# Strassen's scheme for the first large product of an attention-and-MoE kernel, from the third token block on

## The chip, the cores and the metric

The kernel runs on one core of one Trainium2 chip. The metric is device time in microseconds of one execution, lower is better; a time that is given for a kernel is the median of its runs. The core has a matrix engine (TensorE, "PE" in the profile, with its weight loads apart as "PEld"), VectorE (DVE), ScalarE (ACT), GpSimd (POOL) and SyncE (SP), which here issues nearly all transfers. Each engine works through its own list of instructions in order, and the engines wait for each other by semaphores. TensorE writes its results to PSUM, eight banks of 512 float32 columns on 128 partitions; the other data lie in SBUF.

## The reference

An attention without a score matrix feeds a two-layer network without experts' routing. All is float32.

```python
q_s = softmax(q over head_dim);  k_s = softmax(k over seq)      # (8 batches, 8 heads, 576, 64)
kv  = einsum('bhsd,bhse->bhde', k_s, v)                         # 64 x 64 for each head
att = einsum('bhsd,bhde->bhse', q_s, kv)
x   = att.transpose(0, 2, 1, 3).reshape(4608, 512)              # a token's heads side by side
h   = x @ w_in                                                  # 512 -> 2048
r   = maximum(h, 0)
g   = s * (r * r) + b
out = g @ w_out                                                 # 2048 -> 512
```

## The kernel before

**Precision.** TensorE takes its operands in a rounded float32 form (F32R). To keep float32 accuracy each operand is split into a high part and the rest: `xh`, `xl` for x, `gh`, `gl` for g, and two halves for each weight. A product is then three matmuls: high by high, high by rest, rest by high.

**Tiling.** The 4608 tokens are nine blocks of 512: block b of the first eight holds 512 of the 576 tokens of batch b, and the ninth holds the 64 that are left of each batch, which go through a DRAM buffer (`xleft`) and are loaded back at the end (`left_over`, line 699). The 2048 columns of w_in are sixteen chunks of 128 (`NFC`). A step t is one block and one chunk, 144 steps in all. It has twelve matmuls for h (`h_parts`, line 726: four chunks of 128 of the 512 inputs, three matmuls each, 512 tokens wide), then the path through relu, square, scale and bias to `gh` and `gl` (`step`, lines 770 to 791: ScalarE 770 and 787, VectorE 785 and 789), and twelve matmuls for the outputs (`o_parts`, line 814: four tiles of 128 tokens, three matmuls each, 512 output columns wide). The outputs of a block accumulate in four PSUM banks over its sixteen steps and leave through `leave` (line 819).

**Weights.** Block 0 loads each chunk of w_in and w_out, cleans and splits it (`conv_w`, line 189), and keeps it in SBUF for all later blocks, w_in's part in `wt[f][:, 0]`.

**Attention.** The x of batches 2 to 7 is made while the big products of earlier blocks run. For a pair of units (a unit is two heads) it loads k, q and v, takes maxima, exponentials and sums, turns q through DRAM, and multiplies: `kv_late` (line 629) gives the 64 x 64 matrices, `x_late` (line 658) gives x. In `x_late` line 676 has four matmuls per unit, two of 320 and two of 256 columns, into a two-bank PSUM tile ("big") and a one-bank one ("sm"); lines 682 and 686 add the halves into `y` by a ScalarE copy and a VectorE sum, and lines 690 and 694 split `y` into `xh` and `xl`. GpSimd takes the subtraction and the scaling of q (575 and 592) and a split of kv (656).

**What sets the order.** The order of instructions is written by a planner (`Order`, line 114). Each stream of work is a generator that yields operations `Op(engine, cost, due, needs, take, free, gives)`. The planner keeps a time per engine, takes the operation that could start first and, among those of the same engine that could start within 0.1 us of it, the one with the smallest `due`. `take` and `free` count buffers ("h" and "big" are PSUM tiles, "g" the pairs of gh and gl, "w" the weight slots), `needs` and `gives` are results. Costs and dues are constants in the code. `begin(pr)` (line 530) is the due of a pair of attention: the first step of its own block, or six steps later for the second pair. The result is one fixed list per engine, SP's list of transfers included.

## Time and profile before

| | before |
|---|---|
| runs | 871.24, 872.84, 873.27 us; median 872.84 |
| profiled execution, span from first to last instruction | 869.5 us |
| TensorE busy | 851.7 us (98%) |
| VectorE, ScalarE, GpSimd busy | 570.8, 416.3, 91.4 us |
| bytes moved | 79.44 MB, mean 91 GB/s |
| granted TensorE clock | 1.000 |

The span is of one profiled execution; no separate time of that execution outside the profile is listed, so it stands beside the runs' times, which are 2 to 4 us longer. "Busy" is the union of an engine's instructions. Matmuls are pipelined and their ends modelled, so a matmul's listed length is longer than the distance from its start to the start of the next; distances between starts tell what TensorE spends. The chain that ended last follows the work back from the last instruction to what released it. A "releaser" of an idle time is what the engine waited for by the semaphores; idle time of an engine off that chain costs nothing.

### The profile page before, as it was taken

Reading aid. Unit: us, or ns where it says so; the run is one execution under the profiler, and the core shown is the slowest. Engines: PE = TensorE matmul, PEld = TensorE weight load, DVE = VectorE, ACT = ScalarE, POOL = GpSimd, SP = SyncE. Lnnn points to the kernel's source line nnn. Section 1 sums busy time; section 2 is a strip of 40 time slices with the busy share of each in tenths; the row PEclk is TensorE's granted clock in tenths of the full one; section 3 lists DMA queues with packets and bytes.
Section 4 is the critical chain, followed back from the end, with each engine's and each line's share of the span. In section 5 each row is a group of like instructions: output and inputs, shape, how many; then the busy total and the mean of one; then the engine's idle time right before and its main releaser. Section 6 shows DMA issues by size and latency. Waiting matters only on the chain.

```text
span 869.5 us, 11637 instructions
## 1 busy us (share of the span) xinstructions
PE 851.7 (98%) x4367; PEld 701.9 (81%) x4367; DVE 570.8 (66%) x916; ACT 416.3 (48%) x694; POOL 91.4 (11%) x117
## 2 busy tenths in 40 slices
PE   7799999999999999999999999999999999999997
PEld 6578887888888888888888888888888888888886
DVE  6999997596877777686677658785855322232222
ACT  5989864544554545353545354444544322222222
POOL 1000002021102111111021202020200010000000
PEclk9999999999999999999999999999999999999999
DMA  8994134424433334342433242432311000000001
GB/s 232 308 378 136 26 86 118 127 74 97 137 82 89 83 119 100 90 92 78 130 89 83 89 130 75 96 89 82 77 61 52 33 16 1 1 30 19 1 1 48
DMA packets 109991, 79.44 MB, mean 91 GB/s; under 512 B 60656, under 2 KB 103664, under 8 KB 109808
## 3 DMA queue, kind: packets, MB, share of 16 engines
q1 hardware_dynamic: 108496, 77.60, 31.8%
q10 hardware_dynamic: 1440, 1.12, 0.4%
q8 instruction: 34, 0.56, 0.3%
q14 instruction: 21, 0.17, 0.1%
HBM read 60.29 MB, written 18.40 MB: 91 GB/s over the span
## 4 chain that ended last, share of the span: by engine, by line
PE 92%; DVE 4%; DMA 1%; SPq 1%; issue 1%; ACT 0%; ACTq 0%; DVEq 0%
PE acc L814 44%; PE h L726 44%; PE kv L299 2%; PE xp L676 1%; PE xq L676 1%; DMA k<-in_k_dram 1%; DVE low L216 1%; DMA st<-in_moe_w_in_dram 0%; DVE st L213 0%; PE xp L440 0%; DVE w L223 0%; DMA v<-in_v_dram 0%; SPq L288 0%; DVE low L206 0%; DVE st L211 0%
## 5 line engine op out<-in xcount | busy, mean ns | idle before, releaser
L726 PE MATMUL h<-x,w 128*128 128x512 f32 x1728 | 420.2, 391 | 2.4 <-ACT r L770 1.2
L726 PEld LDWEIGHTS h<-x,w 128*128 128x128 f32 x1728 | 322.7, 188 | 71.6 <-ACT r L770 1.9
L814 PE MATMUL acc<-w,gh 128*128 128x512 f32 x1152 | 357.8, 392 | 0.8 <-ACT gh L780 0.8
L814 PEld LDWEIGHTS acc<-w,gh 128*128 128x128 f32 x1152 | 214.0, 188 | 45.6 <-ACT gh L780 1.2
L785 DVE SCALAR_TENSOR_TENSOR r<-r,sb 128x512 f32<-128x512 f32 x135 | 106.1, 786 | 190.1 <-ACT r L770 189.7
L814 PE MATMUL acc<-w,gl 128*128 128x512 f32 x576 | 224.5, 390 | 0.6 <-DVE gl L782 0.6
L770 ACT ACTIVATE r<-h 128x512 f32<-128x512 f32 x143 | 85.5, 598 | 277.3 <-PE h L726 264.9
L789 DVE SCALAR_TENSOR_TENSOR gl<-r,sb,gh 128x512 fp32r<-128x512 f32 x135 | 104.5, 774 | 56.5 <-ACT gh L787 55.2
L787 ACT ACTIVATE gh<-r,sb 128x512 fp32r<-128x512 f32 x135 | 97.7, 724 | 84.8 <-DVE r L785 84.4
L814 PEld LDWEIGHTS acc<-w,gl 128*128 128x128 f32 x576 | 108.1, 188 | 23.8 <-DVE gl L782 1.1
L575 POOL TENSOR_TENSOR q<-q,qm 128x640 f32<-128x640 f32 x24 | 33.7, 1406 | 161.4 <-DVE qm L573 161.4
L592 POOL TENSOR_TENSOR qe<-qe,qr 128x640 f32<-128x640 f32 x24 | 32.3, 1347 | 65.8 <-DVE qr L588 43.7
L682 ACT COPY y<-xp 64x320 f32<-64x320 f32 x48 | 20.2, 420 | 13.8 <-PE xp L676 13.4
L686 DVE TENSOR_TENSOR y<-xp,y 64x320 f32<-64x320 f32 x48 | 23.5, 489 | 3.4 <-ACT y L682 2.5
L562 ACT ACTIVATE k<-k 128x640 f32<-128x640 f32 x24 | 17.7, 737 | 15.1 <-DVE k L524 12.3
L596 DVE STREAM_TRANSPOSE q<-qe 128x640 f32<-128x640 f32 x24 | 19.9, 831 | 5.2 <-POOL qe L592 5.2
L299 PEld LDWEIGHTS kv<-v,k 128*64 128x64 f32 x600 | 18.7, 137 | 5.1 <-issue 4.4
L656 POOL TENSOR_TENSOR spare<-kvf,spare 128x256 fp32r<-128x256 f32 x12 | 10.1, 844 | 118.6 <-issue 112.8
L613 DVE TENSOR_TENSOR qhl<-qT,qhl 64x640 fp32r<-64x640 f32 x24 | 20.6, 860 | 1.1 <-ACT qhl L610 0.4
L686 DVE TENSOR_TENSOR y<-xq,y 64x256 f32<-64x256 f32 x48 | 20.3, 422 | 1.0
L299 PE MATMUL kv<-v,k 128*64 128x65 f32 (+1 forms) x600 | 20.8, 224 | 0.0
L200 ACT ACTIVATE low<-st 128x1024 int32<-128x1024 uint32 (+1 forms) x17 | 18.9, 1111 | 3.2 <-DVE w L223 1.9
(124 smaller groups left out, 619.6 us busy)
## 6 DMA issues: line engine op xcount, KB each, us to landing
st<-in_moe_w_in_dram SPq DMA_DIRECT2D x16, 512.0 KB, 8.7
st<-in_moe_w_out_dram SPq DMA_DIRECT2D x16, 512.0 KB, 9.1
out_dram<-o SPq DMA_DIRECT2D x16, 512.0 KB, 2.7
turned<-q SPq DMA_DIRECT2D x24, 320.0 KB, 2.3
qT<-turned SPq DMA_DIRECT2D x48, 160.0 KB, 3.0
k<-in_k_dram SPq DMA_DIRECT2D x14, 512.0 KB, 4.2
q<-in_q_dram SPq DMA_DIRECT2D x14, 512.0 KB, 5.3
v<-in_v_dram SPq DMA_DIRECT2D x56, 128.0 KB, 4.8
```

Source lines behind the costliest of these rows:

```text
L299: nc.tensor.matmul(kv[h * D:(h + 1) * D, i], kt[:, i, h, n], vt[:, 2 * i + h, n], start=(n == 0), stop=(n == NT - 1))
L575: nc.gpsimd.tensor_tensor(out=qt, in0=qt, in1=bc(qm, [P, 2, NT, D]), op=ALU.subtract)
L592: nc.gpsimd.tensor_tensor(out=qe_, in0=qe_, in1=qr, op=ALU.mult)
L613: nc.vector.tensor_tensor(out=t[half[1 - h], h], in0=qT[half[h]], in1=t[half[h], h].bitcast(F32), op=ALU.subtract)
L682: nc.scalar.copy(y[half[h], at], parts[h][a][half[1 - h]])
L686: nc.vector.tensor_tensor(out=y[half[h], at], in0=parts[h][a][half[h]], in1=y[half[h], at], op=ALU.add)
L726: nc.tensor.matmul(hp_, w[:, j, c, :], x[:, c, :], start=(c == 0 and i == 0), stop=(c == NP - 1 and i == 2))
L770: nc.scalar.activation(r, hp_, AF.Relu)
L785: nc.vector.scalar_tensor_tensor(out=r, in0=r, scalar=s_col, in1=r, op0=ALU.mult, op1=ALU.mult)
L787: nc.scalar.activation(gh, r, AF.Identity, bias=b_col)
L789: nc.vector.scalar_tensor_tensor(out=gl, in0=r, scalar=b_col, in1=gh.bitcast(F32), op0=ALU.add, op1=ALU.subtract)
L814: nc.tensor.matmul(acc[blk, j // 2][:, j % 2], g[:, js], w_, start=(f == 0 and i == 0), stop=(f == NFC - 1 and i == 2))
```

## The change

From block 2 on (`PLAIN = 2`, blocks counted from 0) the h of two chunks, a pair, is computed together. The 512 inputs, the 256 columns of w_in and the 512 tokens are each cut in two, and the four half-by-half blocks of h are formed out of seven products in place of eight, in the Winograd form of Strassen's scheme. A product is six matmuls of 256 columns. Its left side is one of A11, A12, A22 (parts of w_in) or S1 to S4 (sums of them), its right side one of B11, B21, B22 (parts of x) or T1 to T4 (sums of them).

- *Sums of w_in.* In block 1 the needed parts are stored to DRAM (`keep_parts`), the sums are made from them and stored too (`combine`: VectorE two sums, GpSimd four of half width, ScalarE two high parts, GpSimd two rests, for each of eight pairs of chunks). The weight slots of w_in become free slots. In blocks 2 to 8 each product's left side is loaded again from DRAM, two products per transfer of 512 KB (`stream`), at most six transfers ahead (`KEPT`). The slots (16 of the weights, 4 of an x buffer, less one that serves as a third g) hold these loads and the x parts.
- *Sums of x.* `prepare` takes the place of lines 688 to 694: from `y` it makes B and T parts and their splits, on VectorE, ScalarE and GpSimd.
- *Products.* One two-bank PSUM tile, `hset`, has four quarters of 256 columns. The seven products go to quarters 3, 2, 1, 3, 3, 0, 2. Quarter 3 is copied away by ScalarE three times in a pair, after the products 1, 3 and 4 (results u1, u2, u3); products 0 to 6 wait for these and for the row sums.
- *Rows.* `rows_a` adds u3 to quarters 1 and 2 (first chunk), `rows_b` adds u1 and u2 to quarters 0 and 2 (second chunk), on VectorE from PSUM. `square` then does relu and square in one VectorE instruction, scale and bias and gh on ScalarE, gl on GpSimd. Before, this was two ScalarE and two VectorE instructions for a chunk.
- *Outputs.* Same matmuls as before, as a stream of their own with due t + 9; g has three buffers.
- *Attention.* Its dues become a list, `DUE_B`. From block 3 on `x_late` does a unit in two halves with one-bank PSUM tiles "h" and "sm", because `hset` now keeps "big".

The diff, cut to its core:

```diff
+    DUE_S = (11.0, 12.0, 17.0, 17.0, 26.0, 20.5, 26.0, 69.5)
+    DUE_B = (7.5, 8, 16, 28.0, 43.5, 47.0, 55.5, 60, 69.5, 80.0, 81.5, 107.5)
+    S_ON = ('POOL', 'POOL', 'POOL', 'POOL', 'POOL', 'POOL')
+    X_ON = ('POOL', 'POOL', 'POOL', 'DVE', 'POOL', 'DVE')
+    G_ON = ('POOL', 'POOL')
+    DUE_G = -16.0
+    DUE_R = (-16.0, -18.0)
+    DUE_O = 9.0
+    DUE_ST = 2.5
+    PLAIN = 2
+    HP, OPS = NFC // 2, 7
+    KEPT = 6
...
-        bb, hq = divmod(pr, NP // 2)
-        return NFC * bb + PACE * hq
+        return DUE_B[pr - NP]
...
+            for h in range(2):
+                yield Op("PE", 0.29, due - NFC, needs=needs, take=["h", "sm"], gives=[f"xp{u}"] * h, late=WAIT)
...
+                yield Op("ACT", 0.79, due, take=() if h else ["tmp"])
...
+                yield Op("DVE", 0.91, due, free=["h", "sm"], gives=[f"y{u}"] * h)
...
+    def prepare(bb, c, y, due, free, gives):
+        kt, M = c % 2, TB // 2
+        K = raw["K"][:, kt]
+        if c < 2:
+            yield Op("ACT", 0.36, due, needs=["late"])
+            nc.scalar.copy(K[:, M:TB], y[:, 1])
+            yield Op("DVE", 0.42, due)
+            nc.vector.tensor_tensor(out=y[:, 1], in0=y[:, 1], in1=y[:, 0], op=ALU.subtract)
+            yield Op("ACT", 0.6, due, take=["pc"])
+            t = pair_sum(bb, c, "X0")
+            nc.scalar.copy(both(t[:, 0]), y)
...
+            by(X_ON[c]).tensor_tensor(out=both(t[:, 1]), in0=y, in1=both(t[:, 0]).bitcast(F32), op=ALU.subtract)
+            return
+        yield Op("DVE", 0.7, due)
+        nc.vector.tensor_tensor(out=both(K), in0=y[:, 1].unsqueeze(1).to_broadcast([P, 2, M]), in1=both(K), op=ALU.subtract)
...
+    ORDER = ("A11", "S1", "A22", "S2", "S3", "A12", "S4")
+    WITH = {"A11": "B11", "S1": "T1", "A22": "T4", "S2": "T2", "S3": "T3", "A12": "B21", "S4": "B22"}
...
+    def combine(i):
...
+        for j, g in enumerate((f + 1, f)):
+            yield Op("DVE", 0.7, due, needs=["late", f"w{g} 0"], take=() if j else ["F"])
...
+        for n, (out_, x, y, op) in enumerate(sums):
+            yield Op(S_ON[n], on(S_ON[n], 0.85, 0.42), due)
+            by(S_ON[n]).tensor_tensor(out=out_, in0=x, in1=y, op=op)
...
+    def stream(m):
...
+        yield Op("SP", 0.65, NFC * blk + 2 * uses[0][0] + DUE_ST, needs=needs, take=["pc", "ahead"], kb=512, gives=[f"s{m}"])
+        W[m] = slot()
+        nc.sync.dma_start(W[m].bitcast(F32), ws[n].rearrange("p o l e -> p o (l e)"))
...
+    def products(p):
...
+        before = {
+            0: [f"u3 {p - 1}", f"P{OPS - 1} {p - 1}", f"o{t - 3} {NQ - 1}"], 1: [f"row1 {p - 1}"], 2: [f"row2 {p - 1}"], 3: [f"u1 {p}"], 4: [f"u2 {p}"], 5: [f"row2 {p}"], 6: []
+        }
...
+        where = (3, 2, 1, 3, 3, 0, 2)
+        for k, name in enumerate(ORDER):
...
+            yield Op(
+                "PE", 0.71, t - 1, needs=before[k] + x_needs(blk, x) + [f"s{m}"], take=["big"] if p == 0 and k == 0 else (),
+                free=free + ["pc"] * len(gone), gives=[f"P{k} {p}"] + ([f"h{t}", f"h{t + 1}"] if k == OPS - 1 else [])
+            )
...
+            for kt in range(2):
+                xs = x_of(blk, x, kt)
+                for a, b_ in ((0, 0), (0, 1), (1, 0)):
+                    nc.tensor.matmul(out_, w[:, a, kt], xs[:, b_], start=k in (0, 2) and n == 0, stop=n == 5, skip_group_check=True)
+                    n += 1
...
+    def square(t, row, due, eng, free):
+        yield Op("DVE", 0.79, due)
+        nc.vector.scalar_tensor_tensor(out=row, in0=row, scalar=0.0, in1=row, op0=ALU.max, op1=ALU.mult)
+        yield Op("ACT", 0.73, due)
+        nc.scalar.activation(row, row, AF.Identity, bias=b_col, scale=s_col)
+        yield Op("ACT", 0.57, due, take=["g"])
+        G[t] = gh, gl = raw["g"][t % 3]
+        nc.scalar.copy(gh, row)
+        yield Op(eng, on(eng), due, free=free, gives=[f"g{t}"])
+        by(eng).tensor_tensor(out=gl, in0=row, in1=gh.bitcast(F32), op=ALU.subtract)
...
+    def rows_a(p):
...
+        for n, k in enumerate((1, 3, 4)):
+            yield Op("ACT", 0.38, due, needs=[f"P{k} {p}"], gives=[f"u{n + 1} {p}"])
+            V, U = raw["V"][p % 2], raw["U"]
+            nc.scalar.copy(U if n == 2 else V[:, n * M:(n + 1) * M], hset[0][:, 3 * M:4 * M])
+        yield Op("DVE", 0.72, due, needs=[f"P2 {p}"], take=["r"], gives=[f"row2 {p}"])
...
+    def outputs(t):
...
+            yield Op(
+                "PE", 0.68, t + DUE_O, needs=[f"g{t}", f"o{t - 1} {j}"],
...
-            + [step(t) for t in range(NSTEP)]
+            + [step(t) for t in range(PLAIN * NFC)]
+            + [late_()] + [g(i) for g in (keep_parts, combine) for i in range(HP)] + [stream(m) for m in range(NPAIR * OPS // 2)]
+            + [g(p) for p in range(NPAIR) for g in (products, rows_a, rows_b)] + [outputs(t) for t in range(PLAIN * NFC, NSTEP)]
```

The steps of blocks 0 and 1 keep their instructions; `DUE_G` gives those of block 1 an earlier due on ScalarE and VectorE.

More of the change, by code (lines that the diff above doesn't have):

```diff
@@ L741, in step @@
         first = blk == 0
+        due = t + (-2 if first else DUE_G)
         parts = h_parts(t)
@@ L748, in step @@
             hp_ = next(parts)
-        yield Op("ACT", 0.5, t - 2, take=["r", "g"], free=["h"] if t < NSTEP - 1 else ())
+        yield Op("ACT", 0.5, due, take=["r", "g"], free=["h"] if t < NSTEP - 1 else ())
         r, gh, gl = g_tiles(t)
```

255 lines of the change are left out of this document (214 added, 41 removed).

## The prediction

> **What bounds the kernel now.** I read the page first: its busy shares, its transfer rates in 40 slices and its chain of work that ended last.
>
> ```profile
> span 869.5 us, 11637 instructions
> PE 851.7 (98%) x4367; PEld 701.9 (81%) x4367; DVE 570.8 (66%) x916; ACT 416.3 (48%) x694; POOL 91.4 (11%) x117
> GB/s 232 308 378 136 26 86 118 127 74 97 137 82 89 83 119 100 90 92 78 130 89 83 89 130 75 96 89 82 77 61 52 33 16 1 1 30 19 1 1 48
> PE 92%; DVE 4%; DMA 1%; SPq 1%; issue 1%; ACT 0%; ACTq 0%; DVEq 0%
> ```
>
> TensorE is the chain. The profiled execution spans 869.5 us and the runs' median is 872.84, so 3.3 us lie around the span; I make the sum on the span and add 3.3. Next, the chain in order of time (start, length), and windows over blocks 1, 2 and 4 (counted from 0), cut where a block's first h starts.
>
> ```profile
> 138.84 2.72 PE h L726 x12
> 141.56 2.72 PE acc L814 x12
> ```
>
> ```profile
> core 0: us, PE busy (x) PEld busy (x) DVE busy (x) ACT busy (x) POOL busy (x), PEclk, DMA share, GB/s
> 131.91:225.60 93.69, 93.69 (x485) 77.34 (x485) 71.43 (x120) 47.19 (x81) 17.42 (x17) 1.00 0.37 95
> 225.60:317.96 92.36, 92.36 (x482) 76.56 (x480) 68.68 (x117) 43.88 (x77) 14.58 (x15) 1.00 0.38 105
> 410.32:502.68 92.36, 92.36 (x482) 76.56 (x480) 65.69 (x112) 43.16 (x76) 13.91 (x14) 1.00 0.34 92
> ```
>
> Twelve matmuls of 512 columns take 2.72 us, 226.7 ns each; a step is 24 of them, 5.44 us, and sixteen steps are 87.04 of a block's 92.36 us; the rest is attention's matmuls. Two blocks with different vector work agree to 0.01 us: nothing but TensorE sets their length. VectorE has 24 us free in block 2, ScalarE 48, GpSimd 78. So a cut in matmul columns is worth its full time, as long as what Strassen adds elsewhere stays below what is free and does not reach TensorE as a wait.
>
> **What a half-width matmul costs.** The change turns 24 matmuls of 512 columns (h of two chunks) into seven products of six matmuls of 256. The kernel before has 48 matmuls of 256 columns, in attention's x product (L676, "xq"), between ones of 320. TensorE's timeline, the first unit and the end of the last:
>
> ```profile
> 172.18 0.31 PE L676 MATMUL xp<-qhl,spare 128*128 128x320 f32 x1
> 172.33 0.28 PE L676 MATMUL xq<-qhl,spare 128*128 128x256 f32 x1
> 172.45 0.31 PE L676 MATMUL xp<-qhl,spare 128*128 128x320 f32 x1
> 172.59 0.28 PE L676 MATMUL xq<-qhl,spare 128*128 128x256 f32 x1
> 172.71 0.39 PE L814 MATMUL acc<-w,gh 128*128 128x512 f32 x1
> ```
>
> ```profile
> 660.05 0.28 PE L676 MATMUL xq<-spare 128*128 128x256 f32 x1
> 660.17 0.62 PE L726 MATMUL h<-x,w 128*128 128x512 f32 x2
> ```
>
> Starts count, since the lengths hold a modelled drain. From a 256-column start to the next it is 0.12; the mean of all 48 is 0.118. That is more than half of 226.7 (113.3): part of a matmul does not shrink with its columns. I take 0.118, the row of the same width and type, and keep 0.1133 as the lower end. Each of these matmuls has a weight load of its own, hidden at this spacing, so the larger number of loads costs nothing more. The Trainium skill, "TensorE: Matmul & The Clock Gate", section "Back-to-back issue gap", gives N/2.4 + 2.5 ns for a warm matmul, 216 ns at 512 columns; the trace disagrees with its 226.7. By the page's 109 ns at 256 columns the result would be about 832 us.
>
> Removed per pair of chunks: 24 x 0.2267 = 5.44. Added: 42 x 0.118 = 4.96. Saved: 0.484. Seven blocks of eight pairs are 56 pairs: **-27.1 us**. The pair then lasts 10.4 us with its outputs, and a block 88.5.
>
> **What is added beside TensorE.** From the groups (the number behind the busy time is the mean in ns), then from the view of line 785 and of the tile y (min/median/max):
>
> ```profile
> L785 DVE SCALAR_TENSOR_TENSOR r<-r,sb 128x512 f32<-128x512 f32 x135 | 106.1, 786 | 190.1 <-ACT r L770 189.7
> L770 ACT ACTIVATE r<-h 128x512 f32<-128x512 f32 x143 | 85.5, 598 | 277.3 <-PE h L726 264.9
> L789 DVE SCALAR_TENSOR_TENSOR gl<-r,sb,gh 128x512 fp32r<-128x512 f32 x135 | 104.5, 774 | 56.5 <-ACT gh L787 55.2
> L787 ACT ACTIVATE gh<-r,sb 128x512 fp32r<-128x512 f32 x135 | 97.7, 724 | 84.8 <-DVE r L785 84.4
> L656 POOL TENSOR_TENSOR spare<-kvf,spare 128x256 fp32r<-128x256 f32 x12 | 10.1, 844 | 118.6 <-issue 112.8 <-ACT spare L654 5.8
> L694 DVE TENSOR_TENSOR x<-y,x 128x512 fp32r<-128x512 f32 x24 | 20.1, 838 | 0.0
> L449 DVE TENSOR_TENSOR x<-xp,x 128x512 fp32r<-128x512 f32 x8 | 5.5, 681 | 1.6 <-ACT xleft L241 1.4
> L780 ACT CAST gh<-r 128x512 fp32r<-128x512 f32 x8 | 4.9, 618 | 0.2
> L712 POOL TENSOR_TENSOR x<-xleft_all,x 128x512 fp32r<-128x512 f32 x4 | 5.4, 1338 | 72.5 <-ACT x L710 72.5
> ```
>
> ```profile
> L785 DVE SCALAR_TENSOR_TENSOR r<-r,sb x135: 651/753/1459, 38.2 to 854.2; 128x512 f32<-128x512 f32 x135
> ```
>
> ```profile
> L682 ACT COPY y<-xq x48: 363/368/373, 173.7 to 661.5; 64x256 f32<-64x256 f32 x48
> L686 DVE TENSOR_TENSOR y<-xq,y x48: 415/422/428, 176.3 to 662.6; 64x256 f32<-64x256 f32 x48
> L694 DVE TENSOR_TENSOR x<-y,x x24: 628/684/1752, 179.6 to 666.0; 128x512 fp32r<-128x512 f32 x24
> ```
>
> VectorE, block 2 to 5 (mean of the two windows 67.2 us). Removed: 16 x (0.786 + 0.774) = 25.0, and four xl at 0.838, 3.4. Added: 16 row sums from PSUM (nearest L449, 0.681) and 16 squarings (L785's median, 0.753), 22.9; the sums of x, by L694's median and L686: two chunks at 0.42, two at 0.684 + 2 x 0.42, two splits at 0.684, 5.3. That leaves 67.0 in 88.5: no more than before. ScalarE loses 2 x (0.598 + 0.724) and gains three copies at 0.368 and 2 x (0.724 + 0.618) per pair, 1.1 us more, 9 a block beside 44 busy. GpSimd gains 16 + 4 operations at 1.338, 26.8 a block beside 14. All three stay off the path. The sums of w_in are made in block 1 for all pairs: per pair 2 x 0.684 on VectorE (10.9 in all), 4 x 0.844 + 2 x 1.338 on GpSimd (48.4), on ScalarE two casts; VectorE's 71.43 in 93.69 becomes 82.4. Cost nothing, as the steps of block 1 are unchanged and TensorE hides it; if VectorE were full, each us over 93.69 would be lost (first rival). The split of attention's x product into halves, the second waiting until copy and add have emptied the bank, costs TensorE the same four matmuls; its wait is hidden by outputs and products, at worst 0.37 + 0.42 in each of 20 units, 16 us; I take nothing, since queued outputs are ready then.
>
> Waits for TensorE. A product's quarter of the PSUM tile must be emptied before the next use. The end of the kernel shows the hand-over:
>
> ```profile
> 856.06 2.88 PE L726 MATMUL h<-x,w 128*128 128x512 f32 x12
> 858.78 0.39 PE L814 MATMUL acc<-w,gh 128*128 128x512 f32 x1
> ```
>
> ```profile
> 858.98 0.66 ACT L757 ACTIVATE r<-h 128x256 f32<-128x256 f32 x2 [3.30 <-PE h L726]
> ```
>
> ScalarE starts 0.20 after TensorE's next slot begins. So product 4 follows product 3 after 0.20 + 0.37 = 0.57 at the least, less than one output tile (3 x 0.2267 = 0.68); product 5 follows 4 after 0.20 + 0.37 + 0.68 = 1.25 (two tiles); the next pair's product 1 follows this pair's 6 after 0.88, of which product 0 covers 0.71. The loop of products alone is 4.96 + 0.57 + 1.25 + 0.17 = 6.95 of 10.4 us, so 3.4 us a pair are left for queueing behind other work on ScalarE and VectorE (operations of 0.4 to 0.8, five hand-overs), and the outputs wait behind nothing but g. Bounds: none (block 2 to 5 as they are now), or five full operations of 0.8 against 3.4, 0.6 a pair, over the 40 pairs of blocks 2 to 6 that share with attention 24 us. I take 5, nearer to the rows of now: **+5.0**. Below nothing it can't go, as these blocks wait for nothing now.
>
> Pipeline ends. Filling at step 32: products of pair 0 have the outputs of steps 30 and 31 between them, but the first new g comes 4 us after its row: none, to one step's outputs (2.72); **+1.0**. At the end the last row's chain is 0.20 + 0.68 + 0.75 + 0.72 + 0.62 + 1.34 = 4.31, with five hand-overs of 0.04 (below) 4.5, against 2.72 of outputs and two matmuls (0.45) that need gh alone: **+1.3**.
>
> Streams: 3.5 loads of 512 KB in 10.4 us are 176 GB/s on top of 105, 281; in block 1 the 56 stores of 256 KB are 157 GB/s on top of 95, 252; slice 2 of the page moved 378. Off the path, at nothing; late loads are the second rival. New waits hold up what stands behind them: on TensorE, behind a waiting product, the outputs planned after it, and so the g buffers that ScalarE fills; on SP, behind a load that waits for a slot, attention's loads.
>
> Sum: -27.1 + 5.0 + 1.0 + 1.3 = -19.8; 849.7 span, **853.0 us**.
>
> **Rivals.** *GpSimd blocks VectorE* (slower). From the timeline:
>
> ```profile
> 147.13 2.95 POOL L592 TENSOR_TENSOR qe<-qe,qr 128x640 f32<-128x640 f32 x2 [2.56 <-PE h L726]
> ```
>
> ```profile
> 147.67 1.27 DVE L785 SCALAR_TENSOR_TENSOR r<-r,sb 128x512 f32<-128x512 f32 x1 [0.38 <-ACT r L770]
> 148.98 0.73 ACT L787 ACTIVATE gh<-r,sb 128x512 fp32r<-128x512 f32 x1 [1.34 <-DVE r L785]
> ```
>
> A squaring started under a GpSimd operation takes 1.27 in place of 0.753. The Trainium skill, "SBUF — State Buffer", section "Who interferes with whom", says that a VectorE instruction with two SBUF inputs and a GpSimd one that reads SBUF exclude each other, whichever came first; by that rule the trace agrees (1.27), and it speaks against this change. If all new GpSimd time blocked VectorE, block 1 would need 82.4 + 48.4 = 130.8 (+37.1) and blocks 2 to 5 67.0 + 26.8 = 93.8 (+5.3 each, 21): 853.0 - 5.0 + 58 = 906. It decides from about three quarters: block 1 then loses 25.0, as much as the 24.8 left of the gain. Against it: the waits now, 135 x 0.033 at L785 and 24 x 0.154 at L694, are 8.2 us, 9% of GpSimd's 91.4. Chance 0.07.
>
> *Streams late* (slower). The queue's own waits:
>
> ```profile
> SPq L509 <- DVE top L504: 106.5, 12, 13.7
> ```
>
> SP stands up to 13.7 us, 8.9 on average, and loads queue behind that. A load lasts 10.4 / 3.5 = 3.0 us of products: six ahead are 18, enough. If slots let only two be ahead, 12 waits each cost 8.9 - 6 = 2.9, 35 us: 883. It loses from about 2.3 ahead. Against it: twenty slots, and SP takes these waits when it has nothing else. Chance 0.05.
>
> *Copies and sums come late, part of the gain*: 0.4 us a pair over 40 pairs in place of 5.0, 16: 864. For it: five hand-overs a pair where there was one a step; against it the 3.4 us. Chance 0.15.
>
> *Half the columns, half the time*: 42 x 0.1133 = 4.76, saved 0.68, 38.1: 842. Against it the 0.12 between starts. Chance 0.07. The 832 us by the Trainium skill's page on TensorE, above, lie on this side, 10 us further. That fewer products are not made is no case: seven names, six matmuls each, stand in the code.
>
> **How the numbers follow.** Forecast 0.66, with 848 (no waits) to 860 as its own range; late copies 0.15, half time 0.07, blocked 0.07, late streams 0.05. 842 to 867 holds all but the last two and a margin. About 0.3% (2.6 us) is what a measurement tells from no change: faster 0.66 + 0.07 + 0.13 = 0.86, same 0.04, slower 0.10.
>
> **What would show it.** Right: 256-column starts 0.118 apart, 2352 of them, block windows of 88.5 to 89.5 from block 2 on, VectorE near 67 in blocks 2 to 5, the last two blocks shortest. Wrong: PE idle before products ended by ACT or DVE (late copies, and where VectorE's operations are stretched, the lock), by a DMA (streams), block 1 longer than 94 (sums of w_in), or starts under 0.115.

## The result, and the profile after

The changed kernel takes 909.0 us (four runs, 907.4 to 909.5) against 872.4 for the kernel before in runs beside it (four, 871.2 to 873.3): 1.042 times the time before, with a 95% interval of 1.040 to 1.043. It is slower by 37 us where the prediction had it faster by 20. The page of the changed kernel, its first lines and its chain by engine:

```profile
span 907.3 us, 14713 instructions
...
PE 860.1 (95%) x5375; PEld 733.4 (81%) x5375; DVE 660.3 (73%) x976; ACT 510.3 (56%) x932; POOL 339.6 (37%) x301
...
PE 70%; DVE 15%; ACT 6%; issue 3%; DMA 3%; POOL 2%; SPq 1%; DVEq 0%; POOLq 0%; ACTq 0%
```

TensorE held 92% of the chain before and holds 70% now; VectorE went from 4% to 15%. So the chain now runs through other engines for a larger part, that is, TensorE stands more often. Where it stands shows in the windows by block, cut where a block's outputs end (blocks 1 to 4, 7 and 8; columns as in the windows of the prediction):

```profile
137.90:247.55 109.65, 101.10 (x494) 80.39 (x492) 96.12 (x137) 54.40 (x99) 57.57 (x49) 0.95 0.62 168
247.55:356.95 109.40, 100.81 (x695) 86.47 (x694) 93.44 (x136) 62.27 (x121) 66.08 (x55) 0.98 0.85 259
356.95:451.14 94.19, 91.93 (x625) 79.99 (x624) 76.23 (x118) 54.79 (x108) 40.68 (x34) 1.00 0.82 246
451.14:545.62 94.48, 91.67 (x625) 79.95 (x624) 75.01 (x118) 55.18 (x108) 42.23 (x34) 1.00 0.83 247
728.92:817.21 88.29, 85.91 (x530) 75.55 (x528) 34.44 (x44) 37.82 (x70) 28.02 (x21) 1.00 0.52 176
817.21:901.98 84.77, 81.54 (x487) 70.75 (x485) 23.65 (x30) 30.26 (x53) 19.39 (x15) 1.00 0.37 132
```

Cut the same way, the kernel before has 92.36 in each of blocks 1 to 6, and in blocks 7 and 8:

```profile
692.84:779.90 87.06, 87.06 (x386) 72.07 (x384) 26.48 (x33) 24.12 (x38) 5.35 (x4) 1.00 0.03 13
779.90:864.61 84.71, 84.71 (x373) 69.48 (x371) 25.40 (x35) 21.75 (x35) 0.00 (x0) 1.00 0.04 14
```

Blocks 1 and 2 lose 17 us each, and not one later block gains more than 2.2 us (block 5, 90.22), though each has its eight pairs of cheaper products. In blocks 1 and 2 VectorE is busy for 96 and 93 us and the granted clock (the column after GpSimd's) is below 1.

A ledger of TensorE's time helps to keep these apart. It goes by the distances between starts of matmuls: the usual distance of a width belongs to the matmul, what is over it by more than 0.03 is a wait, and what is over it at half clock stands by itself. The last column is an experiment that is told below. The sums leave out some 7.6 us at the end of each execution, behind the last matmul.

| TensorE, us | before | after | e9: three causes removed |
|---|---|---|---|
| h and products | 392.3 | 368.2 | 367.6 |
| outputs | 392.3 | 396.6 | 396.7 |
| attention | 52.5 | 52.8 | 53.7 |
| waits | 24.9 | 74.4 | 40.6 |
| half clock | 0 | 7.6 | 3.4 |

The products did save 24.1 us. Against that waits grew by 49.5, half clock by 7.6, the outputs by 4.3 and attention by 0.3. That makes 37.6, of the 37.8 by which the span grew.

**The waits.** The list of waits, TensorE's weight loads (what waited, for what, us in total, times, longest; the weight load takes a wait first, so its list is the fuller one):

```profile
PEld hset L948 <- ACT late L984: 31.9, 92, 1.1
PEld hset L948 <- DVE row L987: 8.5, 8, 2.6
PEld acc L1117 <- DVE gl L1092: 5.3, 3, 2.5
PEld xp L718 <- DVE y L678: 4.4, 6, 1.6
```

No DMA is among the larger ones: the streamed sums of w_in come in time. The first row is products waiting for L984, the copy of quarter 3 of `hset`. It is there even in the last two blocks, where attention is gone. One pair of block 8 in TensorE's and ScalarE's timeline, products 0 and 1, product 2, the copy u1, product 3, an output tile:

```profile
862.33 1.60 PE L948 MATMUL hset<-w,w 128*128 128x256 f32 x12
...
863.76 0.88 PE L948 MATMUL hset<-slots,w 128*128 128x256 f32 x6
864.68 0.37 ACT L984 COPY late<-hset 128x256 f32<-128x256 f32 x1 [1.52 <-PE hset L948]
...
865.10 0.62 PE L948 MATMUL hset<-w,w 128*128 128x256 f32 x3 [0.46 <-ACT late L984]
...
865.92 0.63 PE L1117 MATMUL acc<-w,gh 128*128 128x512 f32 x2
...
866.39 0.39 PE L1117 MATMUL acc<-w,gl 128*128 128x512 f32 x1
```

ScalarE had been idle for 1.52 us and yet the copy began at 864.68, 0.20 after product 2's end (863.76 + 6 x 0.12 = 864.48), not 0.20 after product 1's at 863.76. Product 3 therefore waits 865.10 - 864.48 = 0.62 us. The planner's list says that u1 needs product 1 (`enumerate((1, 3, 4))`), and orders the work for that. The built kernel does otherwise: in 54 of the 56 pairs u1 starts after product 2's last matmul, though that writes quarter 1 in the other bank; in the two others it starts before product 2 does. This is as if dependences were kept for a PSUM tile as a whole and counted for what is emitted earlier; e5 below puts that to the test. In 22 pairs nothing stands between the products 2 and 3, and in 20 of them TensorE waits 0.62 us or a little more (the other two are those whose copy came early), 12.5 us in all. Such a pair lasts 11.3 us, and 10.6 where the wait is gone (e5 below).

**VectorE stretched.** The groups of the squaring, one for each row of a pair:

```profile
L967 DVE SCALAR_TENSOR_TENSOR late<-late 128x512 f32<-128x512 f32 x56 | 62.5, 1116 | 1.3
L967 DVE SCALAR_TENSOR_TENSOR row<-row 128x512 f32<-128x512 f32 x56 | 45.6, 814 | 1.2
```

The same instruction takes 0.81 us in the mean for one row and 1.12 for the other, which comes while GpSimd makes the first row's gl. Summed over all of VectorE's instructions, the time over each group's fast ones (its tenth percentile) is 98.6 us in blocks 1 to 8, against 15.6 before; 41 of them fall in blocks 1 and 2.

**Half clock.** Five stretches of 3.4 us have a granted clock of 0.5; the kernel before has none until its matmuls are done. Two windows from ahead of such stretches, then the two stretches themselves (the second column of the busy times is TensorE's weight load, the column after GpSimd's the clock):

```profile
195.50:198.90 3.40, 1.03 (x4) 0.30 (x2) 3.28 (x7) 1.30 (x3) 1.05 (x1) 1.00 0.87 279
250.10:253.50 3.40, 1.00 (x7) 0.80 (x7) 3.30 (x6) 1.75 (x4) 1.04 (x2) 1.00 0.70 235
```

```profile
198.90:202.30 3.40, 3.28 (x8) 2.61 (x9) 2.61 (x5) 1.32 (x2) 2.50 (x3) 0.50 0.71 192
253.50:256.90 3.40, 3.40 (x16) 3.40 (x17) 0.65 (x1) 2.35 (x4) 2.42 (x3) 0.50 0.76 238
```

In each of the first two windows lies one of the longest waits of the list above (2.5 for L1092, 2.6 for L987), and 3.4 us at half clock follow: a long wait can be paid again. One of the five stretches (38.4) lies in block 0, ahead of all sums and products; e6's execution below has none there.

### The profile page after: what moved, and what is told of

Its sections match the earlier page's. It is cut to its first block, busy times and chain, and to the rows that moved or that the text cites. A ratio compares the mean times of both kernels' runs of the same rounds, so it can differ in the third digit from the quotient of the medians.

```text
span 907.3 us, 14713 instructions
## 1 busy us (share of the span) xinstructions
PE 860.1 (95%) x5375; PEld 733.4 (81%) x5375; DVE 660.3 (73%) x976; ACT 510.3 (56%) x932; POOL 339.6 (37%) x301
## 3 DMA queue, kind: packets, MB, share of 16 engines
q10 hardware_dynamic: 1440, 1.12, 0.4%
## 4 chain that ended last, share of the span: by engine, by line
PE 70%; DVE 15%; ACT 6%; issue 3%; DMA 3%; POOL 2%; SPq 1%; DVEq 0%; POOLq 0%; ACTq 0%
PE acc L1117 34%; PE hset L948 27%; PE h L1028 6%; PE kv L311 2%; DVE late L967 1%; ACT late L984 1%; DVE y L678 1%; DVE qs L593 1%; DVE row L987 1%; DVE late L775 1%; DVE late L998 1%; DMA st<-in_moe_w_out_dram 1%; DMA slots<-ws 1%; DMA raw<-in_q_dram 1%; DMA mb<-maxima 1%
## 5 line engine op out<-in xcount | busy, mean ns | idle before, releaser
L1117 PE MATMUL acc<-w,gh 128*128 128x512 f32 x848 | 268.0, 398 | 1.1 <-ACT gh L1090 1.1
L948 PE MATMUL hset<-w,w 128*128 128x256 f32 x1644 | 238.4, 287 | 17.5 <-ACT late L984 11.3
L948 PEld LDWEIGHTS hset<-w,w 128*128 128x128 f32 x1644 | 216.0, 191 | 44.3 <-ACT late L984 28.5
L1117 PEld LDWEIGHTS acc<-w,gh 128*128 128x128 f32 x848 | 150.5, 191 | 25.0 <-ACT gh L1090 1.9
L984 ACT COPY late<-hset 128x256 f32<-128x256 f32 x168 | 62.4, 371 | 123.9 <-PE hset L948 123.1
L987 DVE TENSOR_TENSOR row<-hset,late 128x512 f32<-128x512 f32 x56 | 38.6, 689 | 115.1 <-ACT late L984 114.8
L1117 PE MATMUL acc<-w,slots 128*128 128x512 f32 x456 | 119.3, 394 | 0.0
L1028 PE MATMUL h<-x,w 128*128 128x512 f32 x384 | 99.8, 405 | 4.2 <-ACT r L1073 1.7
L1028 PEld LDWEIGHTS h<-x,w 128*128 128x128 f32 x384 | 73.5, 194 | 23.1 <-ACT r L1073 2.9
L1117 PEld LDWEIGHTS acc<-w,slots 128*128 128x128 f32 x456 | 80.8, 189 | 13.8 <-ACT last L1143 0.4
L998 DVE TENSOR_TENSOR late<-hset,late 128x512 f32<-128x512 f32 x56 | 38.6, 688 | 52.5 <-PE hset L948 52.1
L967 DVE SCALAR_TENSOR_TENSOR late<-late 128x512 f32<-128x512 f32 x56 | 62.5, 1116 | 1.3
```

The source lines that it names most:

```text
L948: nc.tensor.matmul(out_, w[:, a, kt], xs[:, b_], start=k in (0, 2) and n == 0, stop=n == 5, skip_group_check=True)
L967: nc.vector.scalar_tensor_tensor(out=row, in0=row, scalar=0.0, in1=row, op0=ALU.max, op1=ALU.mult)
L984: nc.scalar.copy(U if n == 2 else V[:, n * M:(n + 1) * M], hset[0][:, 3 * M:4 * M])
L987: nc.vector.tensor_tensor(out=by_token(row, blk), in0=as_token(both(hset[0][:, M:3 * M]), blk), in1=as_token(U.unsqueeze(1).to_broadcast([ ...
L998: nc.vector.tensor_tensor(out=by_token(row, blk), in0=as_token(hset[0].rearrange("p (a b) -> p a b", a=2)[:, :, 0:M], blk), in1=as_token(b ...
L1028: nc.tensor.matmul(hp_, w[:, j, c, :], x[:, c, :], start=(c == 0 and i == 0), stop=(c == NP - 1 and i == 2))
```

## The experiments

Theory A: the copy u1 waits for product 2, longer than planned, and TensorE stands ahead of product 3. Rival B: the order has no outputs to spare, so the same wait comes back ahead of another product. Theory C: GpSimd's new operations hold up VectorE, the sums of w_in in blocks 1 and 2 and gl in all blocks. Rival D: attention, taken earlier by its new dues, fills VectorE in blocks 1 and 2. A last rival: VectorE simply has too much work of its own there. The kernels e2, e6, e7, e8, e9 and e13 leave out work that the result needs; they price a cause and are not to be used.

### Four edits that let the planner write a new order

The first four kernels changed one thing each and were planned anew. *e1_u1_after_p2* told the planner what the built kernel does:

```diff
-        for n, k in enumerate((1, 3, 4)):
+        for n, k in enumerate((2, 3, 4)):
```

> Edit: the planner is told that the first copy out of quarter 3 (u1) needs product 2, as the built program makes it wait, and no longer product 1; nothing is left out. Theory A (the copy u1 really starts after product 2, and TensorE stands before product 3 because the planner left no output there): the gaps before product 3, 19.5 us in blocks 1 to 8 of the changed kernel, go away, 909 to about 890, and the pairs of the last two blocks fall from 11.28 to about 10.66 us. Rival B (a pair has no output to spare, so the same wait comes back before product 4 or 5): 907 to 911, and the gap is found at another product.

*e2_no_pool_sums* left GpSimd's sums of w_in out of the kernel and of the plan (the two `by(S_ON...)` instructions with their costs).

> Edit: GpSimd's part of the sums of w_in is left out (four sums and two low parts per pair of chunks, 48 operations in all), so the stored S1 to S4 are not the sums; loads, stores, VectorE's and ScalarE's part stay. Theory C (in blocks 1 and 2 VectorE is overfull because GpSimd's sums hold it up): of the 26.7 us of waits and 5.8 us of half clock in these two blocks most goes, 909 to 880 to 886, and VectorE's stretched instructions there fall from 41 us to under 25. Rival D (it is attention's work, taken earlier by its new dues): less than 6 us gained.

*e3_w_sums_dve* gave them to VectorE (`S_ON` six times `'DVE'`).

> Edit: the same 48 operations run on VectorE in place of GpSimd; nothing is left out. VectorE gets 8 x (4 x 0.42 + 2 x 0.68) = 24 us of work, GpSimd loses about 50. Theory C by exclusion: the 15 us by which VectorE's stretch in blocks 1 and 2 exceeds that of later blocks goes, so the sum is +9 us of VectorE time, 905 to 918. If GpSimd's occupancy costs VectorE nothing (C by plain load): +24, 925 to 935. Rival D: no change or slower.

*e4_old_due* gave attention the dues of before (`DUE_B = (32, 38, 48, 54, ... 118)`).

> Edit: attention's dues go back to those of the kernel before (32, 38, 48, 54, ... 118 in place of 7.5, 8, 16, 28, ... 107.5); nothing is left out. Rival D (attention taken earlier fills VectorE in blocks 1 and 2): 15 us or more gained, 885 to 895. Theory C (the sums of w_in do): 903 to 915, since x of block 2 is due at step 32 in either case.

Measured: 921.2, 928.5, 928.7 and 924.9 us, ratios 1.057, 1.065, 1.065 and 1.061 (each interval 0.002 to 0.003 to either side). All four are slower than the changed kernel, even the one that does less work, and e1 and e4 lie outside every range that was expected of them. The windows show why they tell little. In the first, block 8 fell from 84.77 to 80.03, as theory A has it, but block 4 rose from 94.48 to 106.61:

```profile
443.88:550.49 106.61, 97.11 (x637) 84.35 (x636) 76.43 (x123) 55.31 (x110) 40.68 (x35) 0.95 0.73 222
833.88:913.91 80.03, 80.03 (x487) 69.74 (x485) 24.40 (x31) 30.55 (x53) 19.40 (x15) 1.00 0.39 140
```

The planner is one greedy list, so a changed cost or need writes another order for the whole kernel; here the total moved by 12 to 20 us, and these runs don't tell how much of that is the order and how much the edit. From here on, up to e13, the order of the instructions on every engine was held as in the changed kernel, except for the instructions named.

### e5_two_tiles: the order held, hset as two tiles of one bank

```diff
-                hset.append(ps.tile([P, 2, 512], F32, name="hset", tag="big").rearrange("p a b -> p (a b)"))
-            out_ = hset[0][:, where[k] * M:(where[k] + 1) * M]
+                hset.extend(psq.tile([P, 512], F32, name=f"hset{i}", tag=f"q{i}") for i in range(2))
+            out_ = quarter(where[k])
...
+    def quarter(n):
+        M = TB // 2
+        return hset[n // 2][:, n % 2 * M:(n % 2 + 1) * M]
```

The two row sums, which read both banks, became two VectorE instructions of 256 columns each.

> Edit: the PSUM tile hset becomes two tiles of one bank, so that copy u1 (quarter 3) is made to wait for product 1 and no longer for product 2, which writes the other bank; a row sum becomes two VectorE instructions of 256 columns. Nothing is left out, and the order of the instructions on TensorE, ScalarE, GpSimd and SP is the changed kernel's to the last one. Theory A (the built wait, longer than the planned one, leaves TensorE standing before product 3): the gaps before product 3, 19.5 us, go, pairs of blocks 7 and 8 fall from 11.28 to about 10.66 us, 909 to 886 to 894. Rival B (the order is short of outputs, so the wait reappears before product 4 or 5): over 903.

Measured: 891.6 us, ratio 1.022 (1.020 to 1.024), 17.4 under the changed kernel. A pair of block 8 in its timeline, and its windows of blocks 1, 3, 4 and 8:

```profile
837.17 1.59 PE L956 MATMUL hset<-w,slots 128*128 128x256 f32 x12
...
838.60 0.76 PE L956 MATMUL hset<-slots,w 128*128 128x256 f32 x5
...
838.80 0.37 ACT L999 COPY late<-hset 128x256 f32<-128x256 f32 x1 [0.69 <-PE hset L956]
```

```profile
137.88:247.45 109.57, 100.96 (x493) 80.18 (x492) 96.13 (x137) 54.55 (x99) 57.61 (x49) 0.95 0.60 168
...
356.52:448.48 91.96, 91.55 (x625) 79.97 (x624) 79.45 (x134) 54.61 (x108) 40.58 (x34) 1.00 0.87 251
448.48:540.23 91.75, 90.70 (x625) 79.86 (x624) 78.85 (x134) 55.16 (x108) 42.43 (x34) 1.00 0.85 254
...
805.49:885.24 79.75, 79.75 (x487) 70.34 (x485) 28.54 (x44) 30.29 (x53) 19.37 (x15) 1.00 0.39 140
```

The copy starts 0.20 after product 2's first matmul, while that product still runs. In 36 of the 56 pairs the copy now starts before product 2's last matmul, in place of two. The waits between the products 2 and 3 fell from 16.6 us in the whole kernel to 5.2, by the distances between starts (the expectations have 19.5 for the first of these, which this count does not give). Block 8 fell from 84.77 to 79.75, and TensorE is busy in all of it. Theory A holds, for the later blocks; the rest of the 17.4 us is waits at other places. Block 1 and block 2 (109.57 and 109.07) hardly moved, so they have another cause.

### e6_sums_not_issued and e8_no_combine: the sums of w_in, the order held

```diff
-            by(S_ON[n]).tensor_tensor(out=out_, in0=x, in1=y, op=op)
...
-            by(S_ON[4 + j]).tensor_tensor(out=w_tile(g)[:, 1], in0=F[:, j], in1=w_tile(g)[:, 0].bitcast(F32), op=ALU.subtract)
```

> Edit: GpSimd's 48 sums and low parts of w_in stand in the plan but are not issued, so S1 to S4 are wrong; every other engine has the changed kernel's order to the last instruction. Theory C (GpSimd's sums hold VectorE and ScalarE up in blocks 1 and 2): these blocks give back 15 to 28 of their 32.5 us of waits and half clock, 881 to 894. If it is VectorE's own load there: 903 or more.

Measured: 898.9 us, ratio 1.030 (1.028 to 1.032), 10.1 under the changed kernel; less than theory C expected, more than the rival did. The profiled execution is the fastest of the four, 896.0. Its windows of blocks 1 and 2:

```profile
137.10:239.50 102.40, 95.79 (x493) 77.36 (x494) 85.38 (x139) 54.09 (x99) 25.96 (x22) 1.00 0.69 182
239.50:344.80 105.30, 99.86 (x698) 86.51 (x698) 88.87 (x136) 63.09 (x122) 46.42 (x38) 0.98 0.89 271
```

Block 1 lost 7.3 us, block 2 4.1, and the later blocks about 1. Some 6 of the 13 us between the two profiled executions are half clock: one stretch at 0.50 in place of five. VectorE, which had not one instruction less, was busy 10.7 us less in block 1: that is the stretching by GpSimd. The sums also hold up ScalarE, which must wait for them before its casts (first row below); but TensorE's matmuls come in the same order in both kernels, and of the eight waits in blocks 1 and 2 that e6 shortens by over 0.4 us, six, 5.1 us together, ended with VectorE in the changed kernel and none with that cast. GpSimd's gl ended one wait of TensorE itself (second row):

```profile
ACT w L872 <- POOL late L868: 8.7, 4, 3.5
PE acc L1117 <- POOL gl L974: 0.6, 1, 0.6
```

The second kernel left out VectorE's and ScalarE's part of these sums as well.

> Edit: none of the arithmetic of the sums of w_in is issued (VectorE's 16, GpSimd's 48, ScalarE's 16 instructions); the stores and loads stay, with w_in's own parts in place of the sums, so the output is wrong; the rest keeps its order. Theory C in full: blocks 1 and 2 lose nearly all waits beyond those of block 3, 878 to 890, of which GpSimd's part (the run before) is the larger. If attention's earlier dues fill VectorE there (rival D): 900 or more.

Measured: 897.2 us, ratio 1.028 (1.027 to 1.030), well over the 878 to 890 of theory C in full. It is 1.7 us under e6, less than the runs of one kernel differ: the sums' own work on VectorE, 6.3 us of busy time in block 1 (85.38 to 79.07), is nearly free. Block 1 stays at 101.2. Nor is it rival D by amount: in the changed kernel VectorE runs about as many of attention's instructions in block 1 as before (85 against 84), and in block 2 six more (84 against 78). That they come at worse moments is not excluded.

### e7_gl_short: GpSimd's gl, the order held

```diff
-        by(eng).tensor_tensor(out=gl, in0=row, in1=gh.bitcast(F32), op=ALU.subtract)
+        c = slice(0, TB if t < PLAIN * NFC + 3 else 8)
+        by(eng).tensor_tensor(out=gl[:, c], in0=row[:, c], in1=gh[:, c].bitcast(F32), op=ALU.subtract)
```

> Edit: from step 35 on GpSimd computes 8 of 512 columns of each gl, so the output lacks most of that correction; all other engines have the changed kernel's order. By exclusion between GpSimd and VectorE (theory C): VectorE's stretched time falls from 98.6 us to about 60, the squarings' (line 967) from 31.5 to under 10, and the gaps before products 1 and 5 and before outputs shrink, 909 to 896 to 904. If the stretch lies under TensorE's own work: 907 to 910.

Measured: 897.0 us, ratio 1.029 (1.027 to 1.031), 12.0 under the changed kernel. The groups of the squaring:

```profile
L967 DVE SCALAR_TENSOR_TENSOR row<-row 128x512 f32<-128x512 f32 x56 | 44.9, 801 | 1.2
L967 DVE SCALAR_TENSOR_TENSOR late<-late 128x512 f32<-128x512 f32 x56 | 41.7, 744 | 1.3
```

With GpSimd out of its way the squaring of `late` takes 0.744 in place of 1.116, with the same shapes and order, and VectorE's stretched time falls from 98.6 to 46.6 us. The weight load's waits for L987, a row sum, fall from 8.5 us to 3.0. That gl is also ready sooner explains little, since TensorE had waited for it only 0.6 us (above). Theory C holds for both groups of GpSimd's operations, though blocks 1 and 2 stay long without them. The Trainium skill's page "SBUF — State Buffer", section "Who interferes with whom", tells this: a VectorE instruction with two SBUF inputs and a GpSimd one that reads SBUF take turns; the trace agrees.

### e9_all_three: e5, e6 and e7 together

> Two one-bank tiles, GpSimd's 48 operations on w_in left out, and gl cut to 8 of 512 columns from step 35 on, all three at once, the order of all instructions as in the changed kernel (the last two leave work out: the outputs are wrong where they need it). If the three causes are separate, their gains add: 17.4 + 10.1 + 12.0 = 39.5 under the changed kernel, 869 to 870, and blocks 3 to 8 near 89, 89, 88, 89, 84.5, 79.5. If two of them are the same wait seen twice, or a wait taken away at one place comes back at another, less than 33 is gained: 876 or more. Blocks 1 and 2 stay 8 to 10 us each above the 92.4 of the kernel before in either case, since neither single run brought them lower.

Measured: 873.0 us against 871.8 of the kernel before, ratio 1.001 (0.9998 to 1.002). Together 36.0 us are gone, of the 39.5 that the single gains add up to: between the two expectations, and the three causes are nearly separate. That this is close to the 36.6 us between the changed kernel and the one before does not mean that nothing else is wrong: without the three causes the products' gain in the later blocks just pays for what blocks 1 and 2 still lose. Windows of blocks 1 to 4, 7 and 8:

```profile
136.91:240.88 103.97, 97.23 (x493) 78.29 (x492) 85.33 (x137) 53.93 (x99) 25.94 (x22) 0.98 0.66 176
240.88:342.43 101.55, 98.56 (x695) 87.08 (x694) 81.00 (x155) 62.55 (x122) 29.12 (x37) 0.98 0.97 281
342.43:432.31 89.88, 89.88 (x626) 80.26 (x624) 67.61 (x133) 54.82 (x108) 22.66 (x34) 1.00 0.87 257
432.31:522.42 90.11, 89.89 (x625) 80.16 (x624) 67.84 (x133) 55.12 (x108) 23.10 (x34) 1.00 0.87 259
700.24:784.75 84.51, 84.51 (x529) 75.52 (x528) 31.83 (x59) 37.72 (x70) 8.72 (x21) 1.00 0.54 183
784.75:864.49 79.74, 79.74 (x487) 70.31 (x485) 22.82 (x44) 30.28 (x53) 3.03 (x15) 1.00 0.40 140
```

Blocks 3 to 8 are 19 us shorter than before in sum, and full of matmuls: nearly what the prediction had for them (23, ahead of its waits). Blocks 1 and 2 give it all back: 11.6 and 9.2 longer than the 92.36 of before.

### e13_short_sums: VectorE's own new sums too

Made from e9; the sums of F, y, K and T4 were cut to 8 columns (but for the first F and the first T4), for instance

```diff
-        nc.vector.tensor_tensor(out=both(K), in0=y[:, 1].unsqueeze(1).to_broadcast([P, 2, M]), in1=both(K), op=ALU.subtract)
+        nc.vector.tensor_tensor(out=both(K)[:, :, 0:8], in0=y[:, 1, 0:8].unsqueeze(1).to_broadcast([P, 2, 8]), in1=both(K)[:, :, 0:8], op=ALU.subtract)
```

> As the run with all three causes removed, and VectorE's new sums of w_in and of x cut to 8 columns as well (L863, and in prepare the sums y, K and T4; their low parts stay), the order of the instructions unchanged. VectorE loses 15 x 0.66 = 10 us in blocks 1 and 2 for w_in and 4 x 2 x 0.4 + 4 x 0.65 = 6 us a block for x. If VectorE's added work is what makes rows and x late in blocks 1 and 2, their 9.8 and 6.4 us of waits fall to half or less: 861 to 866. If it is the written order (attention, products and outputs placed for times that do not come), they stay: 870 to 873.

Measured: 867.9 us, ratio 0.994 (0.993 to 0.996), between the two expectations. Blocks 1 and 2:

```profile
136.70:238.94 102.24, 97.96 (x493) 79.58 (x492) 76.90 (x137) 53.92 (x99) 25.49 (x22) 0.97 0.67 179
238.94:339.41 100.47, 97.83 (x696) 86.96 (x695) 75.05 (x154) 62.32 (x122) 27.20 (x37) 0.98 0.98 283
```

VectorE lost 8.4 and 6 us of work, and the waits in the two blocks fell from 9.8 and 6.4 to 6.8 and 5.3. So VectorE's own new work is a quarter of these waits; that VectorE has too much work of its own explains little. The other three quarters are left to the order as written, by elimination: no run took that apart.

### Moving the work to VectorE: e10_gl_dve, e11_gl_sums_dve, e12_gl_every_second

All three are made from e5 with its order held, and leave nothing out; gl went from GpSimd to VectorE, then the sums of w_in too, then gl of every second step alone:

```diff
-        by(eng).tensor_tensor(out=gl, in0=row, in1=gh.bitcast(F32), op=ALU.subtract)
+        nc.vector.tensor_tensor(out=gl, in0=row, in1=gh.bitcast(F32), op=ALU.subtract)
```

> Two one-bank tiles and every gl of the products' rows on VectorE in place of GpSimd, at the same place of the written order; nothing is left out. The exclusion theory: GpSimd's gl costs VectorE 52 us of stretching (98.6 to 46.6 when it was cut), gl itself costs VectorE 112 x 0.75 = 84, so VectorE's load grows by about 32 us, 5 a block, which blocks 3 to 8 have free: 884 to 892 against the 891.6 of the two tiles alone, and the squaring back to about 0.8 us. If VectorE's queue is what holds the rows, gl there comes behind other work and the next row sum behind gl: 895 or more, with waits before the outputs ended by VectorE's gl.

> As the run with gl on VectorE, and the 48 operations on w_in on VectorE too; nothing is left out. They are 32 x 0.42 + 16 x 0.75 = 25 us of VectorE, which in blocks 1 and 2 frees 11 + 5 us of stretching (from the run without them). By the exclusion theory blocks 1 and 2 change by less than 3 us each against the run with gl alone moved. If VectorE is simply full in block 1 (101 of 109.6 us), block 1 grows by 5 to 12.

> Two one-bank tiles, gl of even steps on VectorE and of odd steps on GpSimd; nothing is left out. VectorE gets 42 us of gl and loses about half of the 52 us of stretching, so its load grows by 16, 2.5 a block. By the exclusion theory it lies between the two tiles alone (891.6) and the run with all gl on VectorE, and the squaring between 1.27 and 0.8 us in the mean.

Measured: 891.3, 892.2 and 886.9 us; ratios 1.022 (1.021 to 1.024), 1.024 (1.022 to 1.026) and 1.018 (1.016 to 1.020). With gl on VectorE the squaring of `late` is not stretched any more (0.746 us) and the time is that of e5: what taking gl off GpSimd could give, VectorE's doing it costs again. Half and half is 4.7 better than e5, and lies below both its neighbours, not between them as expected. Its groups of the squaring say why:

```profile
L982 DVE SCALAR_TENSOR_TENSOR row<-row 128x512 f32<-128x512 f32 x56 | 45.2, 806 | 1.2
L982 DVE SCALAR_TENSOR_TENSOR late<-late 128x512 f32<-128x512 f32 x56 | 41.4, 739 | 0.4
```

Half of gl stays on GpSimd, and yet neither row is stretched. It was the gl of even steps, the first row of a pair, that met the squaring of `late`; the gl of odd steps meets no squaring. So the whole gain in the squaring is had for half of the added work on VectorE. With the sums of w_in on VectorE block 1 went from 108.1 to 111.9, just over the 3 us that the exclusion theory allowed, and block 2 is at 107.8; but the profiled execution is the slowest of its four (895.0), and by the medians the two kernels differ by 0.9 us.

### e14_port_planned: an order that knows of the exclusion

Made from e5, with gl and the sums of w_in on VectorE, other dues and a few other costs, one more need, and a planner that lets no GpSimd operation and no VectorE operation with two SBUF inputs run at once:

```diff
             t = max(self.at.get(o.eng, 0.0), ready)
+            if o.port:
+                t = max(t, self.at.get("port", 0.0))
...
+                if o.port:
+                    self.at["port"] = end
```

> Two one-bank tiles, sums of w_in and gl on VectorE, other dues, and a planner that lets no operation of GpSimd and no VectorE operation with two SBUF inputs run at the same time; nothing is left out. If the remaining loss is an order written for times without the exclusion, it lies well under the 886.9 of the best order so far: 870 to 880, and with luck under 872. If VectorE and GpSimd simply have too much work that excludes each other in blocks 1 and 2, writing it down better gains less than 5 us: 882 to 890, and blocks 1 and 2 keep over 105 each.

Measured: 885.7 us, ratio 1.016 (1.014 to 1.017), the lowest of those that leave nothing out (e12's interval overlaps it), and 13.6 slower than the kernel before. Blocks 1 and 2:

```profile
139.00:234.66 95.66, 93.02 (x476) 75.10 (x474) 85.53 (x146) 49.48 (x90) 22.19 (x20) 1.00 0.59 171
234.66:352.31 117.65, 103.32 (x707) 91.83 (x707) 103.92 (x206) 66.83 (x130) 22.90 (x23) 0.91 0.82 261
```

Block 1 is nearly whole, and block 2 has what block 1 lost: 213.3 us for both, as in e12 (107.1 + 106.3). The total is in the range of the second expectation. That each of the two blocks would stay over 105 did not come true, only their sum did, and since order, costs and dues all changed at once the run does not tell why.

## Why the prediction was wrong, step by step

**The step that failed is "Waits for TensorE", +5.0.** It held that product 4 follows product 3 after 0.57, and counted 6.95 of 10.4 us in the loop of a pair, with 3.4 left. It took the dependences from the planner's list, where u1 needs product 1, and so left u1 out of the chain. In the built kernel u1 waits for product 2, and where product 3 follows product 2 directly that is 0.20 + 0.37 + 0.05 = 0.62 of TensorE's time. The 3.4 us of room did not help, since the written order has no output at that place; where the planner knew of the wait (e1), block 8 fell to 80.03. e5 priced this at 17.4 us. The prediction's third rival (copies late, 16 us of waits in place of 5.0) had nearly this size, but hand-overs and queueing as the reason, not a dependence on another product. In all, waits grew by 49.5 us and half clock by 7.6, where the sum had 7.3 for waits and ends.

**"Cost nothing" for the sums of w_in in block 1, and gl on GpSimd taken as off the path.** Removing them gained 10.1 (e6) and 12.0 (e7). The sum had nothing for them, and the rival that did was held unlikely since VectorE waited for 9% of GpSimd's time before. Measured: GpSimd's busy time grew by 248 us, and VectorE's stretched time by 83, a third. What the share of before could not show: now the gl of a pair's first row comes when its second row is squared, by the order of the pair itself. The first rival (906 us, chance 0.07) hit the total by accident: it put all 58 us on this lock, of which the runs show 22 at most, half clock behind the waits included.

**The chances** treated the rivals as excluding one another. Here the lock and the late copies both came: 853 + 22 + 17 = 892, and the rest up to 909 is the 20 of the last paragraph below, less the 3.5 by which the single gains exceed the joint one.

**The matmuls, -27.1.** They gave 24.1 (368.2 against 392.3): the distance of the 256-column starts is 280.9/2352 = 0.1194 in place of 0.118, and 2352 x 0.0014 = 3.3 us account for the 3.0 that are short. Half the columns at half the time, the fourth rival, is out. What was not foreseen: the first five or so output matmuls behind a run of products start 0.230 to 0.235 apart (865.92 to 866.39 for two, in the rows above) in place of 0.227, 4.3 us in all; why is not shown.

**Blocks 1 and 2.** Block 1 was to stay as before, block 2 to take 88.5. They take 109.7 and 109.4, and without the three causes still 104.0 and 101.6. VectorE's load was forecast fairly in block 1 (82.4; 85.4 in e6, where the sums of w_in don't stretch it) and in blocks 3 and 4 (67; 67.6 and 67.8 in e9), but not in block 2: there 67 was forecast, and it has 93.4, and 81.0 in e9. The sums of w_in were taken to be done in block 1; the trace has 17 of GpSimd's 48 instructions for them, and 4 of VectorE's 16, in block 2. Why the two blocks stay long without the three causes, with some 16 us of waits in e9 and 12 in e13, and 3 of half clock behind them, stays open. VectorE's timeline in block 1 of the changed kernel shows the form of such a wait. VectorE has no gap, and L1092, for which TensorE's weight load waits 2.5 us here, stands behind three groups of attention's instructions:

```profile
194.07 1.32 DVE L1088 SCALAR_TENSOR_TENSOR r<-r,sb 128x512 f32<-128x512 f32 x1
195.43 0.99 DVE L678 TENSOR_TENSOR y<-xp,y 64x320 f32<-64x320 f32 x2
196.45 0.85 DVE L607 STREAM_TRANSPOSE q<-qe 128x640 f32<-128x640 f32 x1
197.32 0.86 DVE L678 TENSOR_TENSOR y<-xq,y 64x256 f32<-64x256 f32 x2
198.21 0.75 DVE L1092 SCALAR_TENSOR_TENSOR gl<-r,sb,gh 128x512 fp32r<-128x512 f32 x1
```

**Right:** the streams are off the path (no DMA among the larger waits, second rival out); the last blocks are the shortest; the end of the kernel, +1.3, cost less, for block 8 without the late copy has 0.6 us of waits against 0.4 before. By e9 the forecast's 853 misses 2.4 in the products, 4.4 in the outputs, 1.2 in attention and some 12 in waits and half clock beyond the 7.3 that it had for waits and ends: 20 in all, the 873.0 that was measured.

## What to carry to other kernels

Where a gain is 0.5 us in a loop of 10, read every dependence of that loop in the built kernel, not in the plan: two quarters of one PSUM tile in two banks were one object for the waits, and two tiles were worth 17 us. When work moves to GpSimd, ask which VectorE instructions with two SBUF inputs will run at that moment; the share seen before the change says nothing of that. Moving back only what collides (e12) did better here than moving all or nothing. And compare kernels with the order of instructions held, since a planner that writes a new order can hide effects of this size.

## What was not expected of the hardware

TensorE need not stand for a whole stretch to lose its clock. Five windows of 3.4 us in the changed kernel in which it was listed as busy for 1.0 to 2.0 us (two of them in the rows above) were each followed by 3.4 us at 0.50; in the kernel before there was no such stretch while matmuls ran. The Trainium skill, "TensorE: Matmul & The Clock Gate", Part 1, gives this half clock after an idle window of about 3.4 us; the length agrees with the trace, but here the window was a third to over a half busy. No clear limit comes out of these runs: a window with 1.9 us at 31.6 in the changed kernel was followed by the full clock. Both waits of over 2 us in the changed kernel had a stretch at half clock behind them, which costs up to 3.4 / 2 = 1.7 us more; in e9 the wait for the same gl was as long (2.48 us from start to start), and the full clock (1.00) followed.
